# Issuing untiled groups of matmuls as four column tiles, in runs that share a tiling

## The chip, the cores and the metric

The kernel runs on one core of one Trainium2 chip. The core has a matrix engine (TensorE, called PE in the profile, with PEld for its weight loads), a vector engine (DVE), a scalar engine (ACT), a general engine (POOL) and a queue that issues transfers (SP). The metric is the device time of one execution in microseconds; a kernel's time is the median of its runs.

## The reference

Four layers follow one another on 2048 tokens of 448 features: a layer of attention with a recurrent memory, a gated MLP, the same attention again, the same MLP again, each on a layer norm of its input and added to it. What matters is the attention: it walks over 64 segments of 32 tokens, and 8 memory rows that one segment's output leaves are the first rows of the next segment's input, so that the segments form a chain.

```python
for s in range(n_seg):
    h = jnp.concatenate([mem, xs], axis=1)           # 8 memory rows + 32 tokens
    q, k, v = ...                                     # h times Wq, Wk, Wv; 16 heads of 256
    p = softmax(where(mask, q k^T * scale, -1e9))
    o = jnp.einsum('bhte,hed->btd', p v, Wo)
    mem = o[:, :M, :].copy()                          # the next segment's memory
    outs.append(o[:, M:, :])
...
x = x + A(layernorm(x)); x = x + B(layernorm(x))      # and the same two once more
```

## The kernel before

At the start it multiplies Wq with Wk and Wv with Wo once (`A`, `Bsb`), so that attention needs no separate q, k and v. After that there are two kinds of work.

**The chain** (`chain`, one call for each of 72 steps) advances the memory rows alone. A step handles one segment of the first attention layer and, seven steps behind, one of the second, in the same instructions. It is a string of dependent pieces: `fn` at L891 multiplies the memory by `A`; DVE and ACT turn the result into `uT`; `sc` at L1088 makes scores; softmax on DVE and ACT; a transpose of the probabilities at L1121; `yy` at L1145 and L1148; the copy `YTm`; `oo` at L932 multiplies by `Bsb`; ACT and DVE split the result into a high and a low half, `Ohi` (L940) and `Olo` (L941); `cols` at L951 turns these into columns; from them come `mT` and with it the next step's L891.

**The tiles** of 128 tokens (`att_group`, `norm`, `glu_units`, `glu_down`) are the bulk: L1234 (`Ug`), scores L1260, transposes L1279, `yy` again, output L1309; layer-norm transposes L1180; the gated MLP L1333 and L1352. They fill TensorE while the chain waits for the other engines.

**Tilings of the TensorE array.** Every group of matmuls given to `add` has a `mode`, a number for how it cuts the 128x128 array. Mode 0 is the whole array: L951, L1088, L1121, L1180, L1260, L1279, L1309, L1352, and the preparation's transposes and products. Mode 1 is four column tiles of 128x32: L932, with four weight loads and four matmuls for each pass, each to its own 32 partitions of one PSUM bank. Mode 2 is two row tiles (L1234, L1333, L1145, L1148), mode 3 two column tiles (a few products), and mode 4 eight tiles of 64x32 (L891).

**The order.** A planner written in Python (`_Sched.schedule`) lays out every engine's instructions before the program is emitted. TensorE's order is not chosen there: `line()` reads it, group by group, from the string `LINE`. For the other engines the planner takes, each time that an engine is free, the ready piece of highest priority; it picks ACT or DVE for copies that either can do (`EV`), and PSUM banks by when they come free. It does so against its own times: a matmul of n columns costs `max(n, 54) / 2.4 + 2.5` ns (`mm_cost`), a group in another mode than the one before costs `TURN = 94.0` ns more, and where TensorE would idle over 300 ns it inserts filler matmuls (L1367, mode 0).

```python
if mode is not None and o.mode != mode:
    turn = self.TURN
mode = o.mode
```

So the modes enter the plan as well as the program.

## Time and profile before

| what | value |
|---|---|
| median of three runs | 1512.64 us (1510.69 to 1513.66) |
| profiled execution, its own time | 1510.83 us |
| its span, first to last instruction | 1509.0 us |
| PE busy | 1486.1 us, 98% of the span, 36,999 matmuls |
| weight loads (PEld) busy | 1059.0 us, 70%, beside the matmuls |
| DVE busy | 1167.8 us, 77% |
| ACT busy | 891.9 us, 59% |
| POOL busy | 120.1 us, 8% |
| granted TensorE clock | 1.000 |

A busy time is the union of an engine's instructions. Matmuls are pipelined: the 0.35 us shown for one with 448 columns is its way through the array, while the next starts 0.19 us later. What a matmul costs in a stream is therefore the distance from start to start, and a sum over durations would count the same time twice.

### The profile page before, as it was taken

How to read it: one execution, taken by the hardware profiler on the slowest of the kernel's cores; microseconds unless marked ns; L12 is line 12 of the kernel's file. 1: busy time of each engine (PE TensorE's matmuls, PEld its weight loads, DVE VectorE, ACT ScalarE, POOL GpSimd, SP SyncE). 2: the span in 40 equal slices, each digit the busy share in tenths (PEclk: the TensorE clock that was granted, in tenths of full speed). 3: DMA queues.
4: the chain of work that ended last, by engine and by line, in shares of the span. 5: the costliest groups of instructions: out<-in, count | busy, mean ns of one | idle time of the engine just before them, and what ended most of it. 6: DMA issues, size and time to landing. Idle time of an engine off the chain costs nothing.

```text
span 1509.0 us, 82702 instructions
## 1 busy us (share of the span) xinstructions
PE 1486.1 (98%) x36999; PEld 1059.0 (70%) x36999; DVE 1167.8 (77%) x3574; ACT 891.9 (59%) x2407; POOL 120.1 (8%) x483
## 2 busy tenths in 40 slices
PE   7999999999999999999999999999999999999999
PEld 5657666666767777777767677777768777677776
DVE  6767788788888888687877788788877788688764
ACT  8775465566555656565655556566555556555543
POOL 1000000010000010000000010010100000010000
PEclk9999999999999999999999999999999999999999
DMA  8512100000000000000000000000000000000000
GB/s 244 169 30 74 40 8 12 11 9 8 8 5 12 11 8 15 4 18 4 18 5 8 14 9 14 4 18 6 17 6 8 14 8 15 5 8 8 11 6 14
DMA packets 60658, 34.08 MB, mean 23 GB/s; under 512 B 31744, under 2 KB 60176, under 8 KB 60304
## 3 DMA queue, kind: packets, MB, share of 16 engines
q1 hardware_dynamic: 60304, 28.80, 7.4%
q8 instruction: 291, 4.77, 1.3%
q14 instruction: 63, 0.52, 0.1%
HBM read 21.36 MB, written 1.84 MB: 15 GB/s over the span
## 4 chain that ended last, share of the span: by engine, by line
PE 95%; DVE 2%; ACT 1%; DMA 1%; issue 1%; SPq 0%; POOL 0%; DVEq 0%
PE psG L1234 17%; PE psG L1309 17%; PE psG L1333 11%; PE psC L932 10%; PE psC L891 8%; PE psG L1352 5%; PE psG L891 4%; PE psG L1145 3%; PE psG L722 3%; PE psG L1260 3%; PE psC L1088 2%; PE psC L1145 2%; PE psG L709 1%; PE psG L932 1%; PE psG L1180 1%; PE psC L951 1%
## 5 line engine op out<-in xcount | busy, mean ns | idle before, releaser
L1234 PE MATMUL psG<-HT,A 64*128 64x128 bf16 x4924 | 287.2, 216 | 1.0 <-issue 0.6
L1309 PE MATMUL psG<-Bsb,YT 128*128 128x448 bf16 x1344 | 286.2, 353 | 0.0
L1234 PE MATMUL psG<-HX,A 64*128 64x128 bf16 x3693 | 267.6, 216 | 0.0
L1234 PEld LDWEIGHTS psG<-HT,A 64*128 64x128 bf16 x4924 | 235.7, 94 | 14.0 <-issue 8.3
L424 ACT ACTIVATE Ug<-psG 64x128 bf16<-64x128 f32 (+2 forms) x456 | 160.7, 372 | 63.7 <-PE psG L1234 54.7
L1234 PEld LDWEIGHTS psG<-HX,A 64*128 64x128 bf16 x3693 | 195.2, 94 | 0.1
L1309 PEld LDWEIGHTS psG<-Bsb,YT 128*128 128x128 bf16 x1344 | 118.1, 97 | 97.9 <-issue 7.8
L1333 PE MATMUL psG<-G,glu 64*128 64x128 bf16 x5880 | 185.6, 216 | 0.7 <-issue 0.4
L1333 PEld LDWEIGHTS psG<-G,glu 64*128 64x128 bf16 x5880 | 171.8, 94 | 11.2 <-issue 8.4
L932 PE MATMUL psC<-Bsb,YTm 128*32 128x448 bf16 x3304 | 167.3, 353 | 0.3
L1065 DVE STREAM_TRANSPOSE uT<-Usb 128x384 bf16<-128x384 bf16 x280 | 154.6, 559 | 6.1 <-ACT Usb L424 1.8
L891 PE MATMUL psG<-A,mT 64*32 64x448 bf16 x4004 | 144.8, 350 | 0.5 <-issue 0.5
L891 PE MATMUL psC<-A,mT 64*32 64x448 bf16 x3836 | 140.8, 350 | 0.1
L424 ACT ACTIVATE YT<-psG 128x448 bf16<-128x448 f32 x254 | 128.3, 544 | 10.3 <-PE psG L1148 8.9
L932 PEld LDWEIGHTS psC<-Bsb,YTm 128*32 128x32 bf16 x3304 | 82.8, 97 | 65.1 <-ACT YTm L424 1.6
L427 DVE CAST Ug<-psG 64x128 bf16<-64x128 f32 (+2 forms) x250 | 104.8, 430 | 16.0 <-PE psG L1234 11.8
L940 ACT ACTIVATE Ohi<-psC 128x448 bf16<-128x448 f32 x122 | 46.9, 384 | 116.4 <-PE psC L932 85.5
L1338 ACT ACTIVATE hG<-psG 128x512 bf16<-128x512 f32 (+1 forms) x125 | 67.7, 543 | 72.3 <-PE psG L1333 65.6
L891 PEld LDWEIGHTS psC<-A,mT 64*32 64x32 bf16 x3836 | 71.9, 92 | 50.0 <-DVE mT L427 3.9
L941 DVE TENSOR_TENSOR Olo<-psC,Ohi 128x448 bf16<-128x448 f32 x122 | 51.4, 422 | 71.5 <-ACT Ohi L940 70.8
L1339 DVE TENSOR_TENSOR hG<-hG,psG 128x512 bf16<-128x512 bf16 (+1 forms) x116 | 70.7, 614 | 29.5 <-ACT hG L1338 28.0
L1352 PE MATMUL psG<-glu,hG 128*128 128x448 bf16 x420 | 92.4, 352 | 0.0
(223 smaller groups left out, 2874.4 us busy)
## 6 DMA issues: line engine op xcount, KB each, us to landing
HR<-xn SPq DMA_DIRECT2D x128, 32.0 KB
Tsb<-Rsb SPq DMA_DIRECT2D x256, 1.5 KB
Tsb<-Rsb SPq DMA_DIRECT2D x256, 2.0 KB
Bsb<-in_A_Wq_dram SPq DMA_DIRECT2D x8, 384.0 KB
Bsb<-in_A_Wk_dram SPq DMA_DIRECT2D x8, 384.0 KB
HR<-Rsb SPq DMA_DIRECT2D x126, 1.5 KB
HR<-Rsb SPq DMA_DIRECT2D x126, 2.0 KB
X<-in_A_x_dram SPq DMA_DIRECT2D x16, 112.0 KB
```

The lines of the kernel that those rows point to most:

```text
L424: return E.activation(out, i, ACT.Copy, scale=1.0 if scale is None else scale)
L427: return E.tensor_copy(out, i)
L891: i = E.matmul(ub[v].ap()[32 * j:32 * j + 32, 0:D], lhsT=self.mT[rw, WHERE[b], first:first + 32], rhs=cols, start=(b == 0), stop=(b == 6), ...
L932: x = E.matmul(bo.ap()[32 * j:32 * j + 32, 0:D], lhsT=self.YTm[:, q, :], rhs=self.Bsb[:, chunks[q], :], start=(i == 0), stop=(i == 13), ti ...
L1065: self.s.add("dve", 578, lambda E, e, out=out, hh=hh: E.transpose(out, heads[hh]), r=[("Usb", 2 * half + v) for v in range(2)], w=[f"uT{ha ...
L1145: return E.matmul(ps[:, n * q:n * q + n], lhsT=HR[rows, 128 * q:128 * q + 128], rhs=PT, start=True, stop=True, tile_position=(b, 0))
L1234: i = E.matmul(ub[v].ap()[:, 128 * n:128 * n + 128], lhsT=self.A[rw, b, a0:a0 + 128], rhs=HT[rw, WHOLE[b], :, 0:SEG] if CROSS[b] is None e ...
L1309: i = E.matmul(bo.ap()[:, 0:D], lhsT=YT[:, c, :], rhs=self.Bsb[:, 14 * g + c, :], start=(g == 0 and c == 0), stop=(g == 3 and c == 13))
L1333: i_ = E.matmul(two[v].ap()[:, 128 * c:128 * c + 128], lhsT=self.Wgu[rw, b, f0:f0 + 128], rhs=G[rw, WHOLE[b] if CROSS[b] is None else 4 + ...
L1338: s.add("act", 170 + 0.833 * N, lambda E, e, dst=dst, z=two[0], N=N: E.activation(dst, z.ap()[:, 0:N], ACT.Relu), r=[two[0]], w=[("hG", i, ...
L1339: s.add("dve", dv_cost(N), lambda E, e, z=two[1], N=N, dst=dst: E.tensor_tensor(dst, dst, z.ap()[:, 0:N], ALU.mult), r=[two[1]], w=[("hG", ...
L1352: i_ = E.matmul(bk.ap()[:, 0:D], lhsT=hG[:, c, :], rhs=self.Wd[:, c, :], start=(c == 0), stop=(c == NFC - 1))
```

## The change

`add` gets a parameter `also`: further modes in which a group may be issued. Eight kinds of untiled group get `also=(1,)`: L951, L1088, L1121, L1180, L1260, L1279, L1309 and L1352. `line()` now walks over TensorE's order once it is read, and gathers consecutive groups as long as they have a mode in common; when a group comes that shares none with the run so far, the run is closed and each of its groups gets the smallest mode that all of them allow. A run of groups that may all be untiled stays untiled; a run with an L932 in it becomes mode 1 throughout. A new function `packed` issues a matmul untiled, or, in mode 1, as four matmuls on 32 columns of the weights each, with the same moving data, to four times 32 partitions of the output. The strings `LINE` and `ORDER` stay as they are.

```diff
-        return out + left
+        out += left
+        run, have = [], None
+        for o in out + [None]:
+            may = {o.mode, *o.also} if o else set()
+            if have is not None and not have & may:
+                for x in run:
+                    x.mode = min(have)
+                run, have = [], None
+            have = may if have is None else have & may
+            run.append(o)
+        return out
...
-                ins = o.fn(E, eng)
+                ins = o.fn(E, o.mode if o.also else eng)
...
+def packed(E, mode, out, lhsT, rhs, **k):
+
+    if mode != 1:
+        return E.matmul(out, lhsT=lhsT, rhs=rhs, **k)
+    for j in range(4):
+        q = slice(32 * j, 32 * j + 32)
+        i = E.matmul(out[q], lhsT=lhsT[:, q], rhs=rhs, tile_position=(0, 32 * j), **k)
+    return i
...
-                    i = E.matmul(bo.ap()[:, 0:D], lhsT=YT[:, c, :], rhs=self.Bsb[:, 14 * g + c, :], start=(g == 0 and c == 0), stop=(g == 3 and c == 13))
+                    i = packed(E, e, bo.ap()[:, 0:D], YT[:, c, :], self.Bsb[:, 14 * g + c, :], start=(g == 0 and c == 0), stop=(g == 3 and c == 13))
                 return i
-            s.add("pe", mm_cost(*[D] * (hi - lo)), oo, r=yk + bk, w=[bo], alloc=[bo] if (g == 0 and lo == 0) else ())
+            s.add("pe", mm_cost(*[D] * (hi - lo)), oo, r=yk + bk, w=[bo], alloc=[bo] if (g == 0 and lo == 0) else (), also=(1,))
...
```

The other seven kinds of group are edited in the same way, and the planner's costs of a group (`mm_cost`) stay the same in either form.

More of the change, by code (lines that the diff above doesn't have):

```diff
@@ L70 @@
                  "start", "end", "need_inc", "val", "clock", "slot", "seq", "alloc", "mode",
-                 "touch", "busy", "cross", "at")
+                 "touch", "busy", "cross", "at", "also")
 class _Bank:
@@ L121, in part, with add @@
         self.shift = 0.25 * (STEPS.index(ORDER[self.unit]) - 26) if self.unit < len(ORDER) else 0.0
-    def add(self, engs, cost, fn, r=(), w=(), prio=None, dma=0, alloc=(), room=(), mode=0, now=None, busy=None, cross=False, at=0):
+    def add(self, engs, cost, fn, r=(), w=(), prio=None, dma=0, alloc=(), room=(), mode=0, now=None, busy=None, cross=False, at=0, also=()):
         o = _Op()
@@ L131, in add @@
         o.at = at
+        o.also = also
         o.deps = {}
@@ L327, in filler @@
         f.at = 0
+        f.also = ()
         f.idx, f.engs, f.cost, f.eng, f.dma, f.touch, f.mode = -1, ("pe",), {"pe": n * ns}, "pe", 0, [], 0
@@ L950, in cols @@
                     w = O[:, 128 * ((k + 1) % 4):128 * ((k + 1) % 4) + 128]
-                    x = E.matmul(br.ap()[:, 32 * k:32 * k + 32], lhsT=w, rhs=self.Sel[:, :], start=(q == 0), stop=(q == 1))
+                    x = packed(E, e, br.ap()[:, 32 * k:32 * k + 32], w, self.Sel[:, :], start=(q == 0), stop=(q == 1))
             return x
-        s.add("pe", mm_cost(*[32] * 8), cols, r=["Ohi", "Oli", "Oh2", "Ol2", "Sel"], w=[br], alloc=[br], room=MEM + ["mC"], **P)
+        s.add("pe", mm_cost(*[32] * 8), cols, r=["Ohi", "Oli", "Oh2", "Ol2", "Sel"], w=[br], alloc=[br], room=MEM + ["mC"], also=(1,), **P)
         low, upp = slice(0, 64), slice(64, 128)
@@ L1087, in sc @@
                 for k in range(4):
-                    i = E.matmul(psS()[:, c, 0:L], lhsT=self.uT[:, k, row + c].rearrange("p h t -> p (h t)"), rhs=HT[:, k, sg % 4, :], start=(k == 0), stop=(k == 3))
+                    i = packed(E, e, psS()[:, c, 0:L], self.uT[:, k, row + c].rearrange("p h t -> p (h t)"), HT[:, k, sg % 4, :], start=(k == 0), stop=(k == 3))
             return i
         uk = ["uT0", "uT1", "uT2"]
-        s.add("pe", mm_cost(*[L] * (4 * na)), sc, r=uk + [q for c, sg, l in act for q in self.ht_keys(l, sg)], w=[bq], alloc=[bq], **P)
+        s.add("pe", mm_cost(*[L] * (4 * na)), sc, r=uk + [q for c, sg, l in act for q in self.ht_keys(l, sg)], w=[bq], alloc=[bq], also=(1,), **P)
         S_ = lambda: psS()[:, c0:c1, 0:L]
@@ L1120, in middle @@
         bp = self.bank("C", "G")
-        s.add("pe", 56, lambda E, e: E.matmul(bp.ap().bitcast(BF)[:, 0:128], lhsT=m["P"][:, :], rhs=self.ident[:, :], is_transpose=True),
-              r=[k_("P"), k_("P0"), k_("P1"), "ident"], w=[bp], alloc=[bp], **P)
+        s.add("pe", 56, lambda E, e: packed(E, e, bp.ap().bitcast(BF)[:, 0:128], m["P"][:, :], self.ident[:, :], is_transpose=True),
+              r=[k_("P"), k_("P0"), k_("P1"), "ident"], w=[bp], alloc=[bp], also=(1,), **P)
         s.add(EV, ev_cost(128, fast=True), copy_any(m["PT"][0:104, :], lambda: bp.ap().bitcast(BF)[0:104, 0:128]), r=[bp], w=[k_("PT")], **P)
@@ L1179, in tr @@
             for k, o in enumerate(BLOCK):
-                x = E.matmul(pk()[:, k, :], lhsT=xn[:, o:o + 128], rhs=self.ident[:, :], is_transpose=True)
+                x = packed(E, e, pk()[:, k, :], xn[:, o:o + 128], self.ident[:, :], is_transpose=True)
             return x
@@ L1187, in norm @@
             G = self.G2[g]
-            s.add("pe", mm_cost(*[128] * 4), tr, r=xnk + ["ident"], w=[bk], alloc=[bk], room=[("G2", g, v) for v in range(3)])
+            s.add("pe", mm_cost(*[128] * 4), tr, also=(1,), r=xnk + ["ident"], w=[bk], alloc=[bk], room=[("G2", g, v) for v in range(3)])
             s.add(EV, ev_cost(512, fast=True), copy_any(G[:, 0:4, :], pk), r=[bk], w=[("G2", g, 0)])
@@ L1195, in norm @@
         HT, HX = self.HT[l][b], self.HX[l][b]
-        s.add("pe", mm_cost(*[128] * 4), tr, r=xnk + ["ident"], w=[bk], alloc=[bk], room=[("HTx", l, b), ("HX", l, b, 0), ("HX", l, b, 1)])
+        s.add("pe", mm_cost(*[128] * 4), tr, also=(1,), r=xnk + ["ident"], w=[bk], alloc=[bk], room=[("HTx", l, b), ("HX", l, b, 0), ("HX", l, b, 1)])
         for p in range(2):
@@ L1259, in sc @@
                 for k in range(4):
-                    i = E.matmul(psS()[:, sg, :], lhsT=Ug[:, k, sg, :], rhs=HT[:, k, sg, :], start=(k == 0), stop=(k == 3))
+                    i = packed(E, e, psS()[:, sg, :], Ug[:, k, sg, :], HT[:, k, sg, :], start=(k == 0), stop=(k == 3))
             return i
         hk = list(dict.fromkeys(k for q in range(4) for k in self.ht_keys(l, 4 * t + q)))
-        s.add("pe", mm_cost(*[L] * 16), sc, r=uk + hk, w=[bs], alloc=[bs], room=[k_("Tx")])
+        s.add("pe", mm_cost(*[L] * 16), sc, r=uk + hk, w=[bs], alloc=[bs], room=[k_("Tx")], also=(1,))
         mk = self.maskb[:, :].unsqueeze(1).to_broadcast([128, 4, L])
@@ L1278, in pt @@
             for p in range(2):
-                i = E.matmul(bp.ap().bitcast(BF)[:, 128 * p:128 * p + 128], lhsT=Pf[:, 128 * p:128 * p + 128], rhs=self.ident[:, :],
-                             is_transpose=True)
+                i = packed(E, e, bp.ap().bitcast(BF)[:, 128 * p:128 * p + 128], Pf[:, 128 * p:128 * p + 128], self.ident[:, :], is_transpose=True)
             return i
-        s.add("pe", mm_cost(128, 128), pt, r=[("Px", si), "ident"], w=[bp], alloc=[bp], room=["PTx"])
+        s.add("pe", mm_cost(128, 128), pt, r=[("Px", si), "ident"], w=[bp], alloc=[bp], room=["PTx"], also=(1,))
         s.add(EV, ev_cost(256, fast=True), copy_any(PT[0:104, :], lambda: bp.ap().bitcast(BF)[0:104, 0:256]), r=[bp], w=["PTx"])
@@ L1351, in fn @@
                 for c in range(4 * q, 4 * q + n):
-                    i_ = E.matmul(bk.ap()[:, 0:D], lhsT=hG[:, c, :], rhs=self.Wd[:, c, :], start=(c == 0), stop=(c == NFC - 1))
+                    i_ = packed(E, e, bk.ap()[:, 0:D], hG[:, c, :], self.Wd[:, c, :], start=(c == 0), stop=(c == NFC - 1))
                 return i_
-            s.add("pe", mm_cost(*[D] * n), fn, r=[("hG", i, q), f"Wd_{q}"], w=[bk], alloc=[bk] if q == 0 else ())
+            s.add("pe", mm_cost(*[D] * n), fn, r=[("hG", i, q), f"Wd_{q}"], w=[bk], alloc=[bk] if q == 0 else (), also=(1,))
         self.add_x(t, bk)
```

## The prediction

> **What bounds the kernel now.** I read the engines' shares first, then the chain that ended last, then the stretch of the timeline around one output group of the recurrent chain, and at last who waited for whom. The shares and the chain of the page:

> ```profile
> PE 1486.1 (98%) x36999; PEld 1059.0 (70%) x36999; DVE 1167.8 (77%) x3574; ACT 891.9 (59%) x2407; POOL 120.1 (8%) x483
> PE 95%; DVE 2%; ACT 1%; DMA 1%; issue 1%; SPq 0%; POOL 0%; DVEq 0%
> ```

> TensorE is the bound, and 95% of the path to the end lies on it. So each ns that TensorE spends without streaming counts, if nothing else is late when it is saved. The timeline of PE shows such ns:

> ```profile
> 568.15 0.22 PE L1148 MATMUL psG<-PTx,HR 40*128 40x64 bf16 x4
> 568.30 2.83 PE L932 MATMUL psC<-Bsb,YTm 128*32 128x448 bf16 x56
> 571.07 1.12 PE L1309 MATMUL psG<-Bsb,YT 128*128 128x448 bf16 x5
> 572.03 0.56 PE L1260 MATMUL psG<-HT,Ug 128*128 128x40 bf16 x16
> 572.43 1.86 PE L1309 MATMUL psG<-Bsb,YT 128*128 128x448 bf16 x9
> 574.13 0.39 PE L1180 MATMUL psG<-ident,xn 128*128 128x128 bf16 x4
> 574.35 0.28 PE L1279 MATMUL psG<-ident,Px 128*128 128x128 bf16 x2
> ```

> Read the distances of starts. Untiled L1309: 9 in 1.70 us, 189 ns each. L1260: 16 in 0.40 us, 25 ns each. L1180: 4 in 0.22 us, 55 ns each. Between untiled groups nothing is lost. L932 has 14 passes of four matmuls; the trace's starts put the four 3 to 4 ns apart and the passes 189 ns. 14 passes would end at 570.97 (11 ns more for the first pass), but L1309 starts at 571.07: 96 ns pass at the change of tiling. The other changes look the same: from row tiles to L932 90 ns, from untiled to L891 93 ns. Going through PE's starts in order I count 615 changes of tiling, with a median loss of 90 to 96 ns for each pair, some 57 us in all. Beyond these and the streams, TensorE stalls little: after 340 us, 3.7 us in 24 places of over 15 ns.

> The waits of PE, longest in total, name the place that matters here:

> ```profile
> PE psC L951 <- DVE Olo L941: 3.1, 8, 1.0
> ...
> PE psG L932 <- DVE YTm L427: 0.6, 2, 0.4
> ```

> **The change part by part.**

> *Removed: changes of tiling.* With the rule of the diff applied to the groups in the trace's order (fillers left at mode 0), 562 changes remain of 615. 58 go: 44 behind an L932, 14 ahead of one. Five come, all next to fillers, where TensorE waits in any case; I cost these at nothing (0.5 us if that cover were gone). Changes to and from modes 2 and 4 keep their number, since such a group bounds the run in either form. 58 at 94 ns are 5.45 us.

> *What is late next.* L951 waits for L932's result by way of Ohi and Olo, and the 44 lie between these two. What PE does there is the cover of ACT and DVE:

> ```profile
> 352.26 0.55 PE L932 MATMUL psC<-Bsb,YTm 128*32 128x448 bf16 x8
> 352.75 2.06 PE L1309 MATMUL psG<-Bsb,YT 128*128 128x448 bf16 x10
> 354.65 0.18 PE L951 MATMUL psC<-Sel,Ohi 128*128 128x32 bf16 x1
> ```

> ```profile
> 353.44 0.62 DVE L941 TENSOR_TENSOR Olo<-psC,Ohi 128x448 bf16<-128x448 f32 x1 [1.86 <-ACT Ohi L940]
> 354.36 0.22 DVE L941 TENSOR_TENSOR Olo<-psC,Ohi 128x64 bf16<-128x64 f32 x1 [0.29 <-ACT Ohi L940]
> ```

> Ten matmuls of 189 ns and one change cover the way from L932 to Olo's end at 354.58. The shortest distance from Olo's end to L951's start in the trace is 57 ns; here it is 68, so 11 ns are spare. Take the 96 ns away and L951 stalls for 85. I took this spare for each of the 44 (L951's start less Olo's end, less 57), and for the 14 ahead of L932 the like with YTm's end (shortest 52). 33 of the 58 have 94 ns or more and keep all; 6 keep 39 to 90 ns, 402 ns together; 19 have under 20 ns or stall already and keep 0.06 us in sum. Kept: 33 x 94 + 402 + 62 = 3.57 us. What waits behind a stalled L951 on PE is the rest of its stretch and L891; in nothing but the 0.09 us each do these come later than hoped, and not later than now.

> *Added: the packed form.* The runs with an L932 hold 1477 untiled matmuls: 519 of 448 columns (L1309, L1352), 170 of 128 (L1121, L1180, L1279), 508 of 40 (L1088, L1260) and 280 of 32 (L951). Each becomes four loads and four matmuls, 4431 more of each. The 519 take 189 ns in either form, L932 being this very shape: nothing, hidden by the stream itself. For the other 958 no row shows four column tiles with few columns. From below the price is nothing: the tiles start 3 to 4 ns apart, and the first pass of a group is 11 ns longer in L932 and in L1352 alike, so that the four small loads side by side delay their matmuls no more than one whole load does. From above it is a floor for every load and matmul pair: 25 ns in L1260, so 100 ns a pass: 788 x 75 + 170 x 45 = 66.8 us. A nearer row is L1148: two row tiles with 64 columns, two loads and two matmuls in 29 ns, 7 ns an instruction and 56 a pass: 788 x 31 = 24.4 us. It is an upper bound only, as 64 columns alone need those 29 ns. Supply can be read closer: PE's own wait instructions for the next group come 45, 53 and 60 ns after the first load of a group when 20, 24 and 28 instructions lie between, so its sequencer passes some 2 ns an instruction and eight take 16, under 25. I take the row that is nearest in form, L932 with its 3.5 ns between tiles and its equal first pass: 25 ns and at most 1 ns more in the order of issue, 0.5 us for all.

> [...]

> *Moved: the plan of ACT, DVE and the banks.* The planner knows a turn of 94 ns and none in a run, so it plans the others anew around 58 places. Chain pieces go first, yet an engine that has begun a copy finishes it: a conflict costs up to one copy, 0.54 us (ACT, 448 columns). Between L932 and Olo a saved change moves no chain piece, only the copies behind it, and elsewhere the median distance from an operand's end to its group is hundreds of ns. From below: nothing, or a small gain where a stall of 1.2 us (855.97, L951) goes. From above: one such copy at a third of the 58, 10 us. I take 1 us, near the lower end, for the trace's stalls (3.7 us in 1170) show that conflicts are rare. POOL's copies and SP's transfers follow the chain, with POOL 8% busy and the transfers' packets at 7.4% of the DMA engines' span; they move with it, at nothing. The 8862 additional instructions are some 0.5 MB to fetch (the page has 4.77 MB for 82,702), hidden as now; if fetching fell behind, it would show as (c) below.

> Sum: -3.6 + 0.5 + 1.0 = -2.1 us. The profiled execution took 1510.83 us (span 1509.0 and 1.8 around it), so 1508.7; it lay 1.8 us under the median, and on the median of 1512.64 the forecast is 1510.5 us. That is 0.14%; a measurement of this kernel can tell about 0.2%, 3.0 us, from no change.

> **The rivals.**
> (a) *Everything is kept.* The planner finds Ohi and Olo better places and L951 does not stall: 5.45 less 0.5, 1507.7. For it speaks that at 354.1 the second Ohi piece waits for the long Olo, an order that could be otherwise; against it that this order is written in the program.
> (b) *The new plan stalls.* At a third to a half of the 58 places a chain copy finds its engine taken for half a copy, 0.2 to 0.3 us: 4 to 9 us lost, 1513 to 1518. Against it stand the wide distances; for it that 25 of 70 L951 have under 20 ns spare, so that nothing absorbs such a hit. It decides over the sign from 3.1 us on.
> (c) *A floor for each pair* (the other side). Small packed passes cost 56 ns by L1148's rate, 1512.6 - 3.6 + 24.4 = 1533; with 100 ns 1576. It turns the sign from 4 ns a pass on (3.1 us over 788). Against it: L932's starts 3 to 4 ns apart and the 2 ns supply. [...]
> (d) *Nothing happens*: fillers and stalls take back all, or runs form less often than my count; 1512.6.

> **How the numbers follow.** The forecast 0.40 (1509.0 to 1512.2), (a) 0.17, (b) 0.25, (c) 0.13, (d) 0.05. Faster than by 3.0 us: (a) and 0.16 of the forecast's low end, 0.33. Slower by 3.0: (c) and 0.16 of (b), 0.29. The rest, 0.38, is within. The range runs from 1507.0, all 58 kept and packing free, to 1522, past (b); (c) and a sliver lie outside.

> **What would show it.** Right: 562 or so changes of tiling; L1260's and L951's passes in mode 1 at 25 to 27 ns with four tiles each, transposes at 55; L951's idle time before it, now 3.1 us on Olo, up by about 1.7 us; PE's wait for YTm barely up. Wrong: passes of 30 ns or more in mode 1 (c); new PE waits for PTm, uT or mT (b); L951's waits unchanged (a).

## The result, and the profile after

| | before | changed |
|---|---|---|
| median of the runs | 1512.70 us | 1539.72 us (1537.31 to 1541.24) |
| profiled execution, its own time | 1510.83 us | 1537.31 us |
| its span | 1509.0 us | 1535.5 us |
| matmuls | 36,999 | 41,430 |
| changes of tiling | 615 | 562 |

The changed kernel is slower: 1.0179 times the time before, 95% interval 1.0161 to 1.0197, some 27 us. The forecast was 1510.5 us with a range up to 1522. A second measurement gave 1536.63 us and 1.0173 [1.0157, 1.0188]; one run of it, and one of the variant with the limit 8 below, took about twice as long (2958.69 and 3077.18 us) and counts nowhere here. Each ratio is to runs of the kernel before in the same set, whose medians lay between 1509.09 and 1512.70 us.

Lines have moved: L891, L932, L940, L941, L1145, L1234 and L1333 are now L913, L954, L962, L963, L1167, L1256 and L1354. The eight kinds of group that can be packed all carry a line of the helper: L446 where they were issued untiled, L449 where they were issued as four column tiles. In the variants of the changed kernel below these numbers lie up to three higher.

The shares of the engines, the transfer queue for instructions and the chain that ended last, from the page of the changed kernel:

```profile
PE 1499.4 (98%) x41430; PEld 1081.2 (70%) x41430; DVE 1172.2 (76%) x3579; ACT 891.8 (58%) x2402; POOL 120.3 (8%) x483
q8 instruction: 326, 5.34, 1.5%
PE 91%; DVE 4%; ACT 2%; issue 1%; DMA 1%; SPq 0%; POOL 0%; DVEq 0%
```

The instruction queue on the page of before:

```profile
q8 instruction: 291, 4.77, 1.3%
```

TensorE is still the bound, and its busy share hides the loss: busy time rose by 13.3 us only, the span by 26.5. DVE, ACT and POOL are where they were. PE's share of the chain fell from 95% to 91%. The instruction queue (packets, MB, share) moved 35 packets more, of 16 KB each.

What the change set out to remove is gone. The timeline of PE in the changed kernel, at the same pair of groups as the prediction's second timeline (start, duration, line, and the last number is the count):

```profile
360.37 2.83 PE L954 MATMUL psC<-Bsb,YTm 128*32 128x448 bf16 x56
363.03 2.06 PE L449 MATMUL psG<-Bsb,YT 128*32 128x448 bf16 x40
365.03 0.20 PE L449 MATMUL psC<-Sel,Ohi 128*32 128x32 bf16 x4
```

From L954's start to the next group are 2.66 us for 14 passes; it was 2.77 with the turn. And what this gained is given back at once, in the way the prediction worked out for this very place: DVE's timeline has the second `Olo` end at 364.97, so the columns (`Sel,Ohi`) can't start before 365.03.

```profile
364.75 0.22 DVE L963 TENSOR_TENSOR Olo<-psC,Ohi 128x64 bf16<-128x64 f32 x1 [0.29 <-ACT Ohi L962]
```

From the first output matmul to the columns it was 1.90 us (352.75 to 354.65); now it is 2.00.

What is new is in the waits of PE (line, what it waited for: us in total, times, longest us). The changed kernel:

```profile
PE psG L449 <- issue: 3.9, 5, 1.6
PE psC L913 <- issue: 3.6, 4, 1.3
PE psG L1256 <- issue: 2.5, 7, 0.6
PE psG L913 <- issue: 1.9, 3, 0.7
PE psC L1167 <- ACT PTm L436: 1.5, 4, 0.4
PE psC L449 <- DVE Olo L963: 1.3, 3, 0.5
PE psC L1256 <- issue: 1.2, 3, 0.4
PE psC L446 <- DVE Olo L963: 0.7, 4, 0.3
```

The same list before had these three as its longest entries on "issue":

```profile
PE psG L1234 <- issue: 0.6, 2, 0.3
...
PE psG L891 <- issue: 0.5, 1, 0.5
...
PE psG L1333 <- issue: 0.4, 2, 0.2
```

"issue" means that PE stood still and nothing in the profile released it: no operand was late. All entries of this kind sum to 1.7 us before and to 13.9 us now. Two of the largest are at L913 and L1256, groups that the change doesn't touch; they stand behind the packed runs.

The waits view counts only the time after the modelled end of the last matmul. To see the whole loss I took the starts of TensorE's passes in both traces. From each distance between two passes I subtracted the stream time (columns divided by 2.4, plus 2.5 ns, at least 25 ns, which gives the distances of the untiled rows in the trace of before: 189 ns for 448 columns, 55 to 56 for 128, 25 for 40) and 94 ns for a change of tiling. What is left is a gap if it is over 60 ns; it is "with a wait" if the first instruction behind it waits for a semaphore.

| TensorE's time, us | before | changed | difference |
|---|---|---|---|
| stream time | 1403.1 | 1403.0 | 0 |
| changes of tiling (615, 562), 94 ns each | 57.8 | 52.8 | -5.0 |
| gaps with a wait (65, 115) | 15.6 | 23.7 | +8.1 |
| gaps without a wait (27, 61) | 5.7 | 23.5 | +17.8 |
| excess of under 60 ns, all passes | 14.9 | 20.9 | +5.9 |
| first to last matmul | 1497.1 | 1523.9 | +26.8 |

The largest item has no operand behind it. The timeline of PE in the changed kernel shows one such place:

```profile
745.20 0.93 PE L449 MATMUL psG<-glu,hG 128*32 128x448 bf16 x16
745.95 0.70 PE L449 MATMUL psG<-HT,Ug 128*32 128x40 bf16 x64
746.47 0.95 PE L449 MATMUL psG<-glu,hG 128*32 128x448 bf16 x16
...
747.54 0.95 PE L449 MATMUL psG<-Bsb,YT 128*32 128x448 bf16 x16
748.36 0.46 PE L449 MATMUL psG<-HT,Ug 128*32 128x40 bf16 x39
749.70 0.34 PE L449 MATMUL psG<-HT,Ug 128*32 128x40 bf16 x25 [0.88 <-issue]
```

The second group of scores breaks off after 39 of its 64 matmuls, in the middle of a pass, and goes on 1.34 us after that piece started. The fortieth matmul belongs to the same pass as the three before it and reads the same moving data, so no operand can be missing there. The instruction queue has a packet of 16 KB under way here, from 747.37 to 748.43. The next ones start at 751.20, 755.24 and 759.03, 3.8 to 4.0 us apart. From the start of the one at 742.31 to that of the one at 759.03, TensorE starts 1110 loads, matmuls and waits: 66 in a us.

That gives the first theory: the additional instructions come faster than they can be fetched. 35 packets for 8862 more instructions are 253 instructions a packet; before the change, 291 packets for TensorE's 74,629 instructions, its waits included, are 256.

### The profile page after: what moved, and what is told of

It is laid out like the page before. It is cut to its first block, busy times and chain, and to the rows that moved or that the text cites. A ratio compares the mean times of both kernels' runs of the same rounds, so it can differ in the third digit from the quotient of the medians.

```text
span 1535.5 us, 91564 instructions
## 1 busy us (share of the span) xinstructions
PE 1499.4 (98%) x41430; PEld 1081.2 (70%) x41430; DVE 1172.2 (76%) x3579; ACT 891.8 (58%) x2402; POOL 120.3 (8%) x483
## 4 chain that ended last, share of the span: by engine, by line
PE 91%; DVE 4%; ACT 2%; issue 1%; DMA 1%; SPq 0%; POOL 0%; DVEq 0%
PE psG L446 18%; PE psG L1256 16%; PE psG L1354 11%; PE psC L954 10%; PE psC L913 8%; PE psG L449 7%; PE psG L913 4%; PE psG L1167 3%; PE psG L744 3%; PE psC L446 3%; PE psC L1167 1%; PE psG L731 1%; PE psG L954 1%; PE psC L449 1%; PE psG L1170 1%
## 5 line engine op out<-in xcount | busy, mean ns | idle before, releaser
L1256 PE MATMUL psG<-HT,A 64*128 64x128 bf16 x4952 | 290.8, 217 | 2.5 <-issue 1.5
L1256 PE MATMUL psG<-HX,A 64*128 64x128 bf16 x3714 | 271.0, 217 | 1.1 <-issue 1.0
L1256 PEld LDWEIGHTS psG<-HT,A 64*128 64x128 bf16 x4952 | 238.1, 94 | 17.1 <-issue 9.0
L1256 PEld LDWEIGHTS psG<-HX,A 64*128 64x128 bf16 x3714 | 197.8, 95 | 1.9 <-issue 1.9
L446 PE MATMUL psG<-Bsb,YT 128*128 128x448 bf16 x879 | 186.5, 352 | 0.0
L1354 PE MATMUL psG<-G,glu 64*128 64x128 bf16 x5880 | 185.8, 216 | 0.3 <-ACT hG L1359 0.2
L1354 PEld LDWEIGHTS psG<-G,glu 64*128 64x128 bf16 x5880 | 171.9, 94 | 10.9 <-issue 7.3
L954 PE MATMUL psC<-Bsb,YTm 128*32 128x448 bf16 x3304 | 167.2, 353 | 0.3
L913 PE MATMUL psG<-A,mT 64*32 64x448 bf16 x3976 | 147.9, 350 | 1.9 <-issue 1.9
L913 PE MATMUL psC<-A,mT 64*32 64x448 bf16 x3864 | 145.4, 350 | 3.9 <-issue 3.6
L436 ACT ACTIVATE YT<-psG 128x448 bf16<-128x448 f32 x255 | 129.1, 544 | 12.5 <-PE psG L1170 11.5
L954 PEld LDWEIGHTS psC<-Bsb,YTm 128*32 128x32 bf16 x3304 | 83.7, 97 | 63.4 <-ACT YTm L436 1.3
L446 PEld LDWEIGHTS psG<-Bsb,YT 128*128 128x128 bf16 x879 | 77.7, 97 | 61.4 <-issue 1.5
L962 ACT ACTIVATE Ohi<-psC 128x448 bf16<-128x448 f32 x122 | 46.9, 384 | 116.6 <-PE psC L954 80.9
L913 PEld LDWEIGHTS psC<-A,mT 64*32 64x32 bf16 x3864 | 73.3, 92 | 52.8 <-issue 5.2
L963 DVE TENSOR_TENSOR Olo<-psC,Ohi 128x448 bf16<-128x448 f32 x122 | 51.4, 421 | 71.2 <-ACT Ohi L962 70.6
L449 PE MATMUL psG<-Bsb,YT 128*32 128x448 bf16 x1860 | 101.6, 353 | 0.5 <-issue 0.5
L913 PEld LDWEIGHTS psG<-A,mT 64*32 64x32 bf16 x3976 | 76.7, 92 | 28.5 <-issue 7.6
```

The lines of the kernel that those rows point to most:

```text
L436: return E.activation(out, i, ACT.Copy, scale=1.0 if scale is None else scale)
L446: return E.matmul(out, lhsT=lhsT, rhs=rhs, **k)
L449: i = E.matmul(out[q], lhsT=lhsT[:, q], rhs=rhs, tile_position=(0, 32 * j), **k)
L913: i = E.matmul(ub[v].ap()[32 * j:32 * j + 32, 0:D], lhsT=self.mT[rw, WHERE[b], first:first + 32], rhs=cols, start=(b == 0), stop=(b == 6), ...
L954: x = E.matmul(bo.ap()[32 * j:32 * j + 32, 0:D], lhsT=self.YTm[:, q, :], rhs=self.Bsb[:, chunks[q], :], start=(i == 0), stop=(i == 13), ti ...
L963: s.add("dve", dv_cost(w), lambda E, e, to=to, of=of: E.tensor_tensor(lo_[:, to], bo.ap()[:, of], hi_[:, to], ALU.subtract), r=[bo, "Oh" + ...
```

## The experiments

### The packing or the plan

Two kernels part the change's two effects. The first keeps the planner's modes, and so its plan, as before, and issues the runs packed:

```diff
-                    x.mode = min(have)
+                    x.form = min(have)
...
-                ins = o.fn(E, o.mode if o.also else eng)
+                ins = o.fn(E, o.form if o.also else eng)
```

> The plan of ACT, DVE, POOL and the banks is that of before (the planner still sees modes 0); only the emission of the runs is packed. Theory S (supply): the packed forms' additional 8862 instructions come faster than PE's instructions are fetched, and PE stands still in the middle of groups, with nothing to wait for. Then the 61 long gaps without a wait of the changed kernel (23.5 us, against 5.7 before) are here too, at 18 to 28 us, and the time is 1530 to 1540. Theory P (plan): the changed plan of the other engines makes the loss. Then this kernel has turns saved and no loss: 1508 to 1514, gaps without a wait near 6 us.

The second keeps the changed plan and issues everything untiled:

```diff
-                ins = o.fn(E, o.mode if o.also else eng)
+                ins = o.fn(E, 0 if o.also else eng)
```

> The plan is the changed one, the emission untiled as before: 36,999 matmuls. Theory S: gaps without a wait stay near 6 us, the turns come back, 1511 to 1518. Theory P: 1530 or more, with PE's waits for ACT and DVE 15 us or more above before's.

Packing under the old plan took 1529.24 us, 1.0147 [1.0128, 1.0166]. The new plan without packing took 1509.71 us, 1.0009 [1.0000, 1.0018]. Both times lie about 1 us below their ranges; before's median was 1509.09 in this set, lower than in the first. So the plan costs about 1 us, as forecast, and the packing makes the loss. The gaps without a wait say the same: 18.4 us in 47 in the first, 4.2 us in 18 in the second. The gaps with a wait were 21.2 and 15.2 us, so these too came with the packing. At the place shown above, one score group of the first kernel breaks off at the same matmul, under another plan (timeline of PE):

```profile
742.06 0.46 PE L450 MATMUL psG<-HT,Ug 128*32 128x40 bf16 x39
743.63 0.34 PE L450 MATMUL psG<-HT,Ug 128*32 128x40 bf16 x25 [1.11 <-issue]
```

### What a stream of packed passes takes by itself

To the kernel before I added, at the start, four streams on zeros, and ran it once: 512 packed passes of 32 columns, 64 untiled matmuls of 448, 1024 untiled of 32, and 128 packed passes of 448.

```diff
+            for _ in range(512):
+                for j in range(4):
+                    i = E.matmul(wb.ap()[32 * j:32 * j + 32, 0:32], lhsT=hG[:, 32 * j:32 * j + 32], rhs=hG[:, 128:160], start=True, stop=True, tile_position=(0, 32 * j))
+            ...
```

> Before, with a burst of matmuls on zeros at the start, whose result nothing reads: 512 passes of four column tiles with 32 columns (4096 instructions), 64 untiled matmuls of 448 columns, 1024 untiled of 32 columns (2048 instructions), 128 passes of four column tiles with 448 columns (1024 instructions). Theory S: after the first few hundred instructions a small pass of eight instructions settles at 100 to 125 ns (256 instructions for each fetch of 16 KB, one some 3.5 us after another), 50 to 62 us for the 512; the untiled ones at 26 to 29 ns each; the wide passes at 189 ns. Theory T: the small passes take 25 to 33 ns throughout, 13 to 17 us.

The timeline of PE at the 512 packed passes (2048 matmuls and as many loads):

```profile
30.36 2.12 PE L630 MATMUL psC<-hG 128*32 128x32 bf16 x222
35.25 1.23 PE L630 MATMUL psC<-hG 128*32 128x32 bf16 x128 [2.77 <-issue]
40.35 1.35 PE L630 MATMUL psC<-hG 128*32 128x32 bf16 x128 [3.87 <-issue]
45.18 1.39 PE L630 MATMUL psC<-hG 128*32 128x32 bf16 x128 [3.47 <-issue]
49.73 1.23 PE L630 MATMUL psC<-hG 128*32 128x32 bf16 x128 [3.17 <-issue]
53.46 1.23 PE L630 MATMUL psC<-hG 128*32 128x32 bf16 x128 [2.50 <-issue]
57.19 1.23 PE L630 MATMUL psC<-hG 128*32 128x32 bf16 x128 [2.50 <-issue]
```

The stream runs for 222 matmuls and then stops after every 128, that is after every 256 instructions. It is a staircase: 256 instructions pass in some 1.1 us, and the next 256 begin 3.5 to 5.1 us after the last ones began (the 3.5 comes later in the stream), 3.73 in the last two steps shown. In each step there is one packet on the instruction queue. One lasts from 32.82 to 33.90 and the stream goes on at 35.25; the next from 37.84 to 38.86 and it goes on at 40.35. So 512 passes took 59.5 us (30.36 to 89.88), 116 ns a pass, as theory S gave it, where the prediction had 25. 256 instructions in 3.73 us are 69 in a us. The granted clock was 1.0 up to 36.71 us and 0.5 from there to 94.74, so from its second stop on the stream ran at half the clock. The stops are no effect of it: the first (2.77 us) lies wholly at the full clock, and the next stream and the changed kernel, at a clock of 1.0, have blocks at much the same distance.

The first stop came after 444 instructions of the stream, fewer than two blocks of 256 and more than one. So some instructions lay ready ahead of the stream; how many can was not shown beyond that.

The untiled matmuls of 32 columns, 25 ns for two instructions, run at 80 in a us. That is 256 in 3.2 us, and the packets start 3.3 to 3.8 us apart here, at a clock of 1.0: nearly fast enough. By the starts the stream stops five times for 0.25 to 0.53 us; two of the stops show in the timeline of PE:

```profile
104.44 13.98 PE L634 MATMUL psC<-hG 128*128 128x32 bf16 x542
118.79 3.35 PE L634 MATMUL psC<-hG 128*128 128x32 bf16 x128 [0.38 <-issue]
122.52 9.51 PE L634 MATMUL psC<-hG 128*128 128x32 bf16 x354 [0.38 <-issue]
```

The two later stretches start 3.73 us apart, 256 instructions, as in the staircase. So the rate is not one fixed number; it lies around 70 to 80 in a us. The packed passes of 448 columns, eight instructions in 189 ns (42 in a us), didn't stop once. After a stop the first six to eight packed small passes took 25 ns each and the others 33, at either clock; the packed scores of the changed kernel show much the same.

The packets also answer for the gaps in the kernels. I looked at where each gap of over 60 ns ends, with passes told apart a little differently than for the table. In the changed kernel 51 of 60 gaps without a wait (22.3 of 23.0 us) end 1.2 to 1.65 us after the end of a 16 KB packet, as in the burst, though that window covers 10% of the span; all 33 in L913 and L1256 are among them. In the kernel before it is 20 of 26 (4.9 of 5.3 us): it waited for instructions already. Of the gaps with a wait it is 7 of 116 (2.0 of 24.1 us), fewer than chance would give.

### More instructions, but spread thin

Is it the number of instructions that costs, or their density? Before's own wide matmuls of L1309 and L1352, all but the first and last of each sum, were cut in four along their columns, untiled. That adds 10,080 instructions, more than the change does, but at eight in 197 ns.

```diff
+    for j in range(4):
+        q = slice(112 * j, 112 * j + 112)
+        i = E.matmul(out[:, q], lhsT=lhsT, rhs=rhs[:, q], start=False, stop=False)
```

> Plan and tilings of before; each 448-wide matmul of L1309 and L1352 but the first and last of a sum (1680 of 1792) is issued as four untiled ones of 112 columns: 10,080 more instructions, no column tile, no change of tiling saved or added. Four streams of 112 columns take 7.6 ns more than one of 448: 12.8 us. Theory S: that and gaps without a wait of 15 to 30 us, 1530 to 1550. Theory T (the column tiles themselves stall the array, whatever the count): 1523 to 1527, gaps without a wait near 6 us.

It took 1521.55 us, 1.0091 [1.0075, 1.0107], and missed what theory S gave: gaps without a wait were 5.0 us, as before the change, which is what theory T gave for them. The 12.5 us that it lost are stream time, 12.8 us more by the same accounting, since four short matmuls stream longer than one (197 ns against 189). So the number of instructions alone makes no gap. The theory as I had worded it, by count, was wrong. What could still stand was density: instructions cost where they are used up faster than 256 in some 3.5 us for longer than what is already fetched lasts. Theory T stood too, until the half kernel below.

### Wide or small

Two kernels on the old plan pack only the matmuls of 448 columns (519 of them, 42 instructions in a us) or only the other 958.

```diff
-    if mode != 1:
+    if mode != 1 or rhs.shape[-1] != D:
```

> Plan of before; in the same runs only the 519 matmuls of 448 columns are packed, the groups of fewer columns stay untiled. 3114 more instructions, and more changes of tiling: 710 by count, 95 more than before, 8.9 us. Theory S2 (it is the local rate that starves PE: 256 instructions can be fetched in some 3.4 us, and small passes use 8 in 25 to 33 ns): wide passes use 8 in 189 ns and leave no gap: without a wait 4 to 8 us, time 8 to 13 us over before (1.005 to 1.009). Theory N (the number of additional instructions counts): 3114 of 8862 bring 6 us, gaps without a wait near 12 us.

> The reverse: in the same runs the 958 matmuls of 32, 40 and 128 columns are packed, the 448-column ones untiled. 711 changes of tiling by count, 9.0 us more than before; 5748 more instructions. Theory S2: the small passes empty the buffer, and the untiled wide ones refill it faster than packed ones would: gaps without a wait 12 to 20 us, time 18 to 28 us over before (1.012 to 1.019). Theory W (the wide passes starve it): gaps without a wait near 6 us.

The wide ones alone took 1520.72 us, 1.0065 [1.0050, 1.0081]. Their gaps without a wait were 6.7 us. Their loss is 10 us, and it is in the changes of tiling: 710 instead of 615, since now runs are mixed, 8.9 us at 94 ns. The small ones alone took 1532.76 us, 1.0145 [1.0131, 1.0158]. Of the 22 us, 9.0 are again changes of tiling (711), 5.0 gaps without a wait (10.7 us, a little under what I expected), 5.3 excess of under 60 ns, and 1.7 gaps with a wait. So the wide packed passes cost nothing by themselves, and the small ones do. But the 1.0 and 5.0 us that they add to before's 5.7 fall short of the 12.7 of both together (18.4). With both packed, the untiled wide matmuls between the small passes and 149 changes of tiling are gone, and in either the fetching could have caught up. That this is the reason was not tried by itself.

### Half the instructions of the small passes

This one keeps the form and takes out density. It is the packing under the old plan, but where a matmul has 32 or 40 columns only two of the four column tiles are issued. Tilings, runs, waits and every pass stay; four instructions a pass are gone. (A few matmuls at the start set the banks to zero.)

```diff
-    for j in range(4):
+    for j in (0, 1, 2, 3) if rhs.shape[-1] > 40 else (1, 3):
```

> As the packed emission with the plan of before (1.0147, gaps without a wait 18.4 us), but a packed matmul of 32 or 40 columns issues only two of its four column tiles. Left out: half of the rows of those scores and memory columns, which hold what was in the bank. Tilings, passes and the order stay; 3152 of the 8862 additional instructions go, all of them in the small passes, which now use 4 in 25 ns. Theory S2 (the fetch of instructions): gaps without a wait fall to 5 to 11 us, no small pass at 33 ns, 1.001 to 1.008. Theory T (column tiles with few columns stall the array, or the groups behind them, by themselves): gaps stay at 15 us or more, 1.011 or more.

It took 1511.97 us, 1.0005 [0.9996, 1.0014], instead of 1.0147. The gaps without a wait fell from 18.4 to 7.6 us (those at the added start left out), and the passes took 25 ns. The group of scores that broke off above runs through (timeline of PE):

```profile
733.97 0.57 PE L452 MATMUL psG<-HT,Ug 128*32 128x40 bf16 x32
734.46 0.36 PE L916 MATMUL psC<-A,mT 64*32 64x448 bf16 x1
```

It needs 0.49 us to the next group for 16 passes and a change of tiling. The four-tile form needed 1.61 (748.36 to 749.97), and before the change the same group, untiled, 0.49:

```profile
731.06 0.56 PE L1260 MATMUL psG<-HT,Ug 128*128 128x40 bf16 x16
731.55 0.36 PE L891 MATMUL psC<-A,mT 64*32 64x448 bf16 x1
```

So the mere form, column tiles with few columns, doesn't cost. This run alone doesn't part the number of instructions from four tiles side by side, as both are halved; the burst's steps of 256 instructions and the packets ahead of the gaps do. And even then next to nothing is gained, with 53 changes of tiling fewer: 5.0 us of turns went, and 2.6 us of gaps with a wait and 1.9 without one came. The matmuls that set the banks to zero put TensorE's work some 2 us later (the fillers at the start begin at 30.36 instead of 28.36 us). Without them the time would be some 1.2 us under before by this estimate, no more than the noise.

### Packing only where little of it is small

Could the change pay in part? Two kernels leave a run as it was when it has more than 8, or more than 16, matmuls of 32 or 40 columns; the plan follows the new modes. A third has the limit 16 and the old plan. The changed kernel was run again beside the first.

```diff
-                for x in run:
-                    x.mode = min(have)
+                if min(have) != 1 or sum(x.tiny for x in run) <= 8:
+                    for x in run:
+                        x.mode = min(have)
```

> The changed kernel once more, for a time on the same chip as the next three and to stand beside the packed emission with the plan of before (1.0147 of before). Theory: the changed plan alone costs nothing (1.0009), so with packing it costs little either: 1.014 to 1.019, gaps without a wait 18 to 24 us.

> The changed kernel, but a run is packed only where it holds at most 8 matmuls of 32 or 40 columns: 273 matmuls instead of 1477, 595 changes of tiling by count, 20 fewer than before. Theory S2: no small stretch empties the buffer, gaps without a wait 4 to 9 us; 1.9 us of turns saved, half of it lost again in L951's wait: 0.997 to 1.002 of before. Theory P2 (the plan and the packing together cost): 1.004 or more.

> As the run with at most 8 small matmuls, with the bound at 16: 686 matmuls packed, 579 changes of tiling by count, 36 fewer than before, 3.4 us. [...] Theory C (gaps grow with the count of packed matmuls): 686 of 1477 bring 8.3 us, gaps near 14 us, 1.003 to 1.007.

> The packing of the run with at most 16 small matmuls (1.0045 with its own plan, gaps without a wait 6.5 us), with the plan of before. If its loss came from the plan made for the packed forms: 0.997 to 1.001, PE's gaps at waits back from 19.6 to some 16 us. If it came from the packing: 1.003 to 1.006 as there.

| limit | matmuls packed | changes of tiling | time, us (before in the same set) | ratio | gaps without a wait, us | gaps with one, us |
|---|---|---|---|---|---|---|
| none packed (before) | 0 | 615 | 1512.70 | 1 | 5.7 | 15.6 |
| 8 | 273 | 595 | 1509.38 (1510.70) | 0.9993 [0.9984, 1.0002] | 5.2 | 15.7 |
| 16 | 686 | 579 | 1515.01 (1509.53) | 1.0045 [1.0031, 1.0058] | 6.5 | 19.6 |
| 16, old plan | 686 | 579 | 1516.98 (1511.22) | 1.0042 [1.0030, 1.0055] | 11.2 | 19.5 |
| no limit | 1477 | 562 | 1536.63 (1510.70) | 1.0173 [1.0157, 1.0188] | 23.8 | 21.7 |

The limit of 8 is no worse than before, and no better that can be told: 20 changes at 94 ns are 1.9 us, and 1.1 us is what the ratio shows, with an interval that touches 1. The limit of 16 lost 0.45%, within the range of theory C, but its profiled execution had 6.5 us of gaps without a wait where that theory gave near 14; it was the fastest of its runs, 1513.26 us. With the old plan the loss is the same, so it comes from the packing. The growth from 8 to 16 to no limit is steeper than the number of packed matmuls. That fits long dense stretches outrunning the fetching, but doesn't show it: at 16 with its own plan the gaps with a wait grew most, by 4.0 us. No variant beat the kernel before by more than the noise.

## Why the prediction was wrong

**Added: the packed form. This step failed.** The prediction took 0.5 us for it. Measured in the changed kernel, it is 17.8 us of gaps without a wait and 5.9 us of excess within passes, 23.7 in sum. Of the 5.9 us some 3 lie in the packed scores, 1 in the packed columns and 2 in L1256, which is unchanged. How much of the 8.1 us of gaps with a wait belongs to it is open. Three sentences carried the mistake. "Its sequencer passes some 2 ns an instruction and eight take 16, under 25" read the supply from 20 to 28 instructions, few enough to be at hand already; the burst shows 256 at that order of speed (some 4 ns each) and then a stop, so 14 ns each (3.73 us for 256) over a longer stretch. And "some 0.5 MB to fetch, hidden as now" took the volume for the cost: the volume is small, 1.5% of the engines' time, but the 16 KB blocks start 3.5 to 4.0 us apart in the burst once it has settled and 3.8 to 4.0 after the break at 748.36 us, and the share says nothing of that. (The 4.77 MB are TensorE's alone: 291 blocks of 256 for its 74,629 instructions with the waits, not for the 82,702 of all engines.) The prediction did name late fetching, but only as rival (c), longer passes; it came as stops. The burst's untiled matmuls show the limit from the other side: at 80 in a us they just about kept up. And "TensorE stalls little" (3.7 us after 340 us) counted idle time behind modelled ends. By the starts the trace of before has 40 gaps of over 60 ns there, 8.8 us; 18 of them, 4.2 us, are without a wait, and 17 of the 18 end 1.2 to 1.65 us after a packet. It also had 291 packets of 16 KB, 256 instructions each, and TensorE using 49 instructions in a us on the mean (73,998 in 1497 us) where a dense small packed pass uses 240 to 320.

Rival (c) carried the price that came true, 24.4 us and 1533, from L1148's rate of 7 ns an instruction, with a chance of 0.13. That its 24.4 and the measured 23.7 agree is luck, as its mechanism, a floor for each pair, is not what happens: a pass in the 8-pass groups of L951 still takes 25 ns, the packed transposes 56, the wide passes 189, and the halved passes run at 25. Only the packed scores in groups of 16 passes (L1260, 384 passes) showed 33 ns, 4.1 ns an instruction, against the 30 that the prediction named as the sign of (c). Their mean was 32.6, and 384 times 7.6 ns are 2.9 us, a real but small part; the chain's packed scores, in groups of eight, stayed at 25. The rest is a rate over hundreds of instructions, which no single pass shows.

The prediction's second sign of what would be wrong, waits for `PTm`, `uT` or `mT`, is not where the loss is: the wait for `PTm` is 1.5 us in both.

**The engine's neighbours made it dearer.** Most gaps do not stand in the packed groups. Of the 23.5 us, 7.8 lie in L913 and about 7 in L1256, which stand behind a run and are unchanged; the packed scores of L1260 have 4.3. These neighbours leave no room: eight tiles of L913 use 85 instructions in a us (16 in 189 ns) and the row tiles of L1256 72 (4 in 55.8 ns), both at or over the 69 of the burst's packed passes. So a debt from the dense stretch is paid there: all 33 gaps in these two end just after a packet, as said above. Before, with untiled wide matmuls at 10.6 in a us between them, there was more time to catch up, and gaps of this kind were fewer.

**Removed: changes of tiling.** Right: 562 was counted and 562 came, and the place shown above lost its turn (2.77 to 2.66 us).

**What is late next.** Right in kind: the place that the prediction costed at 85 ns given back gave back 100. L951's gaps went from 8 to 26. In size it was less than I said: by the starts they rose from 4.0 to 5.0 us, and the waits view, which counts only after modelled ends, has 2.0 us now against 3.1, not 4.8. In the halved kernel 2.6 of the 5.0 us of turns came back as gaps with a wait, about half instead of the third I allowed, and at more places than L951; in the changed kernel, by the starts, the gaps of `yy` that wait for `PTx` rose from 0.3 to 2.2 us.

**Moved: the plan.** Right: 1.0 us was taken; the plan alone measured 1.0009 [1.0000, 1.0018], 1.4 us.

**What stays open.** The gaps with a wait grew by 8.1 us, by 6.1 when the changed kernel was run again, and by 5.6 under the old plan, so most of it is not the plan. Late instructions hidden behind a semaphore's name can be little of it: the gaps with a wait that end just after a packet hold 2.0 us in all. Most wait for operands: of those after 200 us, 68 of 91 (14.4 of 17.7 us) end within 0.15 us of the event that released them. Which of them the missing turns used to cover was not parted place by place. The changed kernel and the same packing under the old plan (1.0173 [1.0157, 1.0188] and 1.0147 [1.0128, 1.0166], from different sets of runs) differ by less than their intervals tell apart.

## What to carry to other kernels

Before splitting a matmul into tiles that stream side by side, count the instructions in a us of the stretch, its neighbours included, and not only the ns of a pass: here 256 instructions took 3.3 to 4 us to come, so some 70 in a us were free, and a stretch of a few hundred above that is paid for later, often in groups that were not touched (here about 15 of 23.5 us). A packed pass of 448 columns, at 42 in a us, was free; one of 40 columns, at 240, was not, and its price didn't show in its own ns. And a rate read from the first twenty-odd instructions of a group is the rate of what is already there: in the burst 444 ran before the first stop.
